# The first batch's loads and order, its weights' buffer, and the slots of all batches in a two-stage attention and gating kernel

## The chip, the cores and the metric

The kernel runs on one core of a Trainium2 chip. Its time is the device time in microseconds of one execution, and several executions give a median. The profile is of one execution; its times start at the first instruction.

## What is computed

For each of four batches, `x` is 12800 x 128 in f32. First 32 inducing vectors attend to all rows of `x` (softmax over 12800, giving `h`, 32 x 128), then every row of `x` attends to `h` (softmax over 32). The result goes through a gated block: a causal depthwise convolution of 5 taps and a sigmoid give the gate, a 128 x 128 product the value, and a second 128 x 128 product the output. The `moe_` weights arrive as f64.

```
def mab(q, kv):
    s = scale * (q @ kv.transpose(0, 2, 1))
    s = s - s.max(-1, keepdims=True)
    a = np.exp(s)
    a /= a.sum(-1, keepdims=True) + 1e-09
    return a @ kv
h = mab(I, x)
x = mab(x, h)
gate_pre += conv_w[k][None, None, :] * xp[:, k:k + S, :]   # k = 0..4
gate = 1.0 / (1.0 + np.exp(-gate_pre))
return (gate * (x @ w_val) @ w_out)
```

## The kernel before

A batch's 12800 rows are four strips (r = 0 to 3) of 3200, and a strip is cut into chunks c of up to 512 columns (`SIZES`): 128, 256, five of 512 and 256 in batch 0; 480, five of 512 and 160 in the others. A pair of a batch and a chunk covers all four strips side by side, so 4 x n rows.

Per batch there are these steps, each a function that adds operations to a plan:

- `load_xt` (L292) brings a chunk of `x` with channels on the partitions, 1024 KB for 512 columns; `load_xk` (L303) brings the same rows with tokens on the partitions and a column of ones. In batch 0, chunks 0 to 5 have no second load: `make_xk` (L315) transposes them on TensorE (L335) and ScalarE (L340) or VectorE (L342) copies them out.
- `s1` (L349): scores against the inducing vectors on TensorE (L359), copied from PSUM with a running maximum by VectorE (tile `ss`, L367).
- `gmax` (L371), in two halves `gm` and `gn`: the maximum of a group of chunks (`GROUPS`), across partitions by a small product (L385), and back by another (L399).
- `e1` and `h` (L412, L427): exponential on ScalarE, transpose on VectorE (`et`), and the product with the tokens (L437), summed into `H` by VectorE.
- `prep` to `prep_out` (L453 to L616): the groups' `H` are joined (L477) and normalised, `hT` is h transposed (L496), and from it and the weights come the gate's and value's weights `W` and the output's `wo`, each in two f16 halves.
- `s2` (L620): scores against `hT` (L633), then ten steps on VectorE, GpSimd and ScalarE that end in the softmax weights `P`, again in two f16 halves. The last are the cast (L682) and the subtraction on GpSimd (L687); for chunk 0 two memsets on GpSimd follow (L692, L693) that clear the halo of 32 columns.
- `rblock` (L722): one half-chunk of gate products (L707) and value products (L716), then tanh on ScalarE (L769) and gate times value on VectorE (L780).
- `halves` (L786): the result `tg` as two f16 halves: `gh` is cast by VectorE (L794) for strips 1 and 3 and by ScalarE (L796) for 0 and 2; `gl` is a subtraction on GpSimd (L802). `outp` (L806) multiplies with `wo` in three f16 products (L814 to L816), scales on ScalarE and stores.

TensorE runs in the order in which the plan was built: the list `START` for the beginning, then half-chunks of `rblock`, with the steps of the next batch put between them by slots (`FILL`, in half-chunks relative to the start of a batch, and `LEAD`, by how many half-chunks a chunk's `s2` comes ahead). The other engines' order is chosen by `Plan.lay`, which runs the plan forward with the durations in `COST` and takes the ready operation that is due first. SyncE's transfers are ordered in the same way. `BUFS` has the number of buffers for each name: four of `xk`, eleven of `xt`, five of `tg`, four PSUM banks `a` and one each of `g0` to `g3`.

The f64 weights are loaded as integers into a buffer of `xk` (L226) and converted on VectorE by eleven operations (L244 to L257) that work in the rest of that buffer.

Of the kernel before, what the change touches and what calls it, by code (L numbers as in the profile page):

```python
# [36 lines left out]
LAT = 0.12  # L37
PASSES = 6

COST = dict(  # L40
    s=0.867 / 512, h=0.052, unit=0.2135 / 512, out=0.68 / 512, switch=0.13,
    psum=(0.14, 1.05e-3), dve=(0.17, 1.02e-3), act=(0.16, 0.83e-3), pool=(0.19, 1.78e-3),
# [3 lines left out]
class Plan:  # L46
# [7 lines left out]
    def op(self, eng, dur, fn, deps=(), early=0.0, new=(), use=()):  # L54
        i = len(self.ops)
        self.ops.append(dict(eng=eng, dur=dur, fn=fn, deps=[d for d in deps if d is not None], early=early))
        for key in new:
            self.tiles.setdefault(key[0], []).append((i, key))
            assert key not in self.users, key
            self.users[key] = []  # L60
        for key in use:
            self.users[key].append(i)
        return i

    def order(self, pe):
# [38 lines left out]
        for i in pe:  # L104
            nominal[i] = t
            t += ops[i]["dur"]
# [10 lines left out]
    def lay(self, deps, succ, topo, nominal):  # L117
# [18 lines left out]
        while len(seq) < n:  # L136
# [12 lines left out]
            end[i] = start + ops[i]["dur"]  # L149
            free[e] = end[i]  # L150
# [23 lines left out]
def tile_kernel(ctx: ExitStack, tc: tile.TileContext, xt, xk, indT_in, w64, out):  # L174
# [16 lines left out]
    def PE(dur, fn, deps=(), new=(), use=()):  # L191
        i = plan.op("PE", dur, fn, deps, 0.0, new, use)
# [39 lines left out]
    i_const = op("POOL", 2.5, f_const)  # L232

    def weights(after):
        w = {}

        def start():
            w["w4"] = c_["wbuf"][:, K64:3 * K64].bitcast(I32).rearrange("p (a k) -> p a k", a=4)
# [3 lines left out]
            w["b"], w["t"], w["u"] = (w["w4"][:, i] for i in range(3))  # L242
            w["lo"] = w["w4"][:, 3].bitcast(F32)
# [16 lines left out]
        for f in ops:  # L260
            i = op("DVE", 0.37, f, [i], 0.0, [], [("xk", "w")])
# [8 lines left out]
        return op("DVE", 0.1, cmax, [i])  # L270
# [13 lines left out]

    def ago():
# [17 lines left out]
    def load_xk(b, c):  # L303
# [4 lines left out]
        def f():  # L308
            x = sb(pxk, key, [P, n, P + 1], F32, [P, 16, P + 1])
            nc.sync.dma_start(x, xk[b, :, o:o + n * (P + 1)].rearrange("p (i c) -> p i c", c=P + 1))  # L310

        ix[key] = op("SP", n * 66048 / BW, f, [ago()], 0.0, [key])


    def make_xk(b, c, eng):  # L315

        n = SIZES[b][c] // 32
        o = HALO // 32 if c == 0 else 0
        key = ("xk", b, c)
        last = []  # L320

        def ones():
            x = sb(pxk, key, [P, n, P + 1], F32, [P, 16, P + 1])
            G.memset(x[:, :, P:], 1.0)

        i0 = op("POOL", 0.15, ones, [], 0.0, [key])
        for g in range(0, n, 4):
# [9 lines left out]
            def ev(g=g, k=k, tk=tk, e=eng[g // 4 % len(eng)]):  # L337
                dst, src = st[key][:, g:g + k, :P], st[tk][:, :k, :]
# [6 lines left out]
            i = PE(0.109 * k + 0.05, tp, [ix["xt", b, c, 1], i_const], [tk], [("xt", b, c, 1)])  # L345
            last.append(op("ACT" if e == "S" else "DVE", 0.6, ev, [i, i0], 0.0, [], [tk, key]))
        ix[key] = op("NOP", 0.0, lambda: None, last)

    def s1(b, c):  # L349
        n = SIZES[b][c]  # L350
        o = HALO // 32 if c == 0 else 0
        key, ss, mx = ("a", "s1", b, c), ("ss", b, c), ("mx", b)
        new = c == 0

        def f():
            s = pt(key)
            x = st["xt", b, c, 1]
# [3 lines left out]
        i = PE(COST["s"] * n + COST["switch"], f, [ix["xt", b, c, 1], i_ind, i_const], [key], [("xt", b, c, 1)])  # L361
# [7 lines left out]
        ix[ss] = op("DVE", cost("psum", n) + 0.1, g, [i], 0.0, [ss] + [mx] * new, [key] + [mx] * (not new))  # L369

    def gmax(b, g):  # L371
# [9 lines left out]
        i0 = op("DVE", 0.12, f0, [ix["ss", b, c] for c in cs], 0.0, [m1], [("mx", b)])  # L381
# [5 lines left out]
        i1 = PE(0.35, f1, [i0, i_const], [key], [m1])  # L387
# [5 lines left out]
        i2 = op("DVE", 0.25, f2, [i1], 0.0, [mr], [key])  # L393

        def second():
# [5 lines left out]
            i4 = PE(0.3, f4, [i2], [key2], [mr])  # L401
# [6 lines left out]
            ix["ng", b, g] = op("DVE", 0.2, f5, [i4], 0.0, [("ng", b)] * (g == 0), [key2] + [("ng", b)] * (g > 0))  # L408
# [3 lines left out]
    def e1(b, g, c):  # L412
# [7 lines left out]
        i = op("ACT", cost("act", n) + 0.09, f, [ix["ng", b, g]], 0.0, [], [ss, ("ng", b)])  # L420
# [6 lines left out]
    def h(b, g, c):  # L427
        nb = SIZES[b][c] // 32
        cs = GROUPS[b][g]
        key, H = ("a", "h", b, c), ("H", b, g)  # L430

        def f():
            t = pt(key)
            e, x = st["et", b, c], st["xk", b, c]
            for i in range(nb):
                s = i % R
                T.matmul(t[32 * s:32 * s + 32, :P + 1], e[:, 32 * i:32 * i + 32], x[:, i, :],  # L437
                         start=i < R, stop=i >= nb - R)
# [10 lines left out]
        pre = [i] + ([ix[H]] if c != cs[0] else [])  # L449
        ix[H] = op("DVE", 0.28, acc, pre, 0.0, [H] * (c == cs[0]), [key] + [H] * (c != cs[0]))  # L450


    def prep(b):  # L453
# [9 lines left out]
        i0 = op("DVE", 0.25, f0, [ix["ng", b, g] for g in gs] + [i_const], 0.0, [f_], [("ng", b)])  # L463
        i0 = op("ACT", 0.25, lambda: S.activation(st[f_], st[f_], AF.Exp, scale=-1.0), [i0], 0.0, [], [f_])
# [6 lines left out]
        i0 = op("DVE", 0.15 * len(gs), f1, [i0], 0.0, Ds, [f_])  # L471
# [7 lines left out]
        i2 = PE(0.23 * len(gs), f3, [i0] + [ix[k] for k in Hs], [key], Hs + Ds)  # L479
# [7 lines left out]
        ix["hn", b] = op("DVE", 0.45, f4, [i2], 0.0, [("hn", b)], [key])  # L487

    def prep1(b):
# [5 lines left out]
        i = PE(0.2, f5, [ix["hn", b]], [key], [("hn", b)])  # L495
        ix["hT", b] = op("DVE", 0.2, lambda: V.tensor_copy(sb(pb, ("hT", b), [P, M]), st[key][:, :M]), [i], 0.0,  # L496
                         [("hT", b)], [key])

    def prep2(b):
# [7 lines left out]
        i4 = PE(0.3, f4, [ix["hT", b], iw], [key], [("hT", b)])  # L507
# [9 lines left out]
        i = op("DVE", 0.5, g0, [ix["hT", b], iw], 0.0, [gmx, cg], [("hT", b)])  # L517
# [19 lines left out]
        i = op("DVE", 0.6, g2, [i4], 0.0, [vmx, wv], [key])  # L537
# [6 lines left out]
        iv = op("DVE", 0.25, g3, [i, ih], 0.0, [], [wv, w2])  # L544
# [437 lines left out]
```

## Time and profile before

| what | us |
|---|---|
| median of 3 runs | 324.81 (323.74 to 325.12) |
| the profiled execution, its own time | 323.54 |
| its span, first to last instruction | 321.6 |
| DMA traffic over the span | 75.03 MB |
| `gl` on GpSimd, 116 operations | 121.3 busy |
| gate products on TensorE, 1740 | 119.4 busy |
| gate times value on VectorE, 116 | 65.7 busy |
| tanh and output scaling on ScalarE, 116 each | 70.4 and 69.6 busy |

A row of the list of groups reads: line, engine, operation, output and inputs, shape, count, then busy time in us, the mean in ns of one, and the idle time just before them. A row of the timeline reads: start, duration in us, engine, line, what it does, count, and in brackets the idle time before it and what ended that. A row of a stage has the stretch, its length and the busy us (and count) of TensorE's products, TensorE's weight loads, VectorE, ScalarE and GpSimd, then TensorE's granted clock, the DMA engines' share and GB/s. Busy times of single TensorE products overlap.

### The profile page before, as it was taken

To read this page: it belongs to the slowest core of one execution; us is meant where nothing else is said; L and a number is where in the kernel's file an instruction comes from. 1 tells how busy PE (TensorE), PEld (TensorE's weight loads), DVE (VectorE), ACT (ScalarE), POOL (GpSimd) and SP (SyncE) were. 2 spreads that over 40 slices of the span, in tenths; PEclk is the share of its full clock that TensorE was granted. 3 is DMA by queue.
4 is the path that set the end of the run, shared out by engine and by line. 5 is a ranking of instruction groups with operands and counts; after the bars stand their busy time and mean duration, and the time that the engine had idled before them with its cause. 6 is when DMAs were issued, how large, how long until landed. Compare 5 with 4: busy or idle time off the path is not lost.

```text
span 321.6 us, 10290 instructions
## 1 busy us (share of the span) xinstructions
PE 297.3 (92%) x4112; PEld 141.1 (44%) x4112; DVE 259.9 (81%) x629; ACT 214.8 (67%) x406; POOL 210.1 (65%) x233
## 2 busy tenths in 40 slices
PE   8996769999998999999999999999898989999894
PEld 3665535643442446433443446334444334333241
DVE  1578596789988998888998889898999988988452
ACT  3453024577866678679765785788657777879595
POOL 1000044579758685889758777886877698999573
PEclk9997795999999999999999999999997999999798
DMA  7996990863999619958999299523221322233334
GB/s 296 427 416 246 423 418 11 314 231 116 346 408 413 257 67 349 402 204 306 287 412 391 86 316 385 186 92 129 96 102 67 132 110 94 106 124 130 130 133 172
DMA packets 24527, 75.03 MB, mean 233 GB/s; under 512 B 2848, under 2 KB 7456, under 8 KB 19488
## 3 DMA queue, kind: packets, MB, share of 16 engines
q1 hardware_dynamic: 24336, 74.37, 60.8%
q8 instruction: 32, 0.52, 0.7%
q14 instruction: 15, 0.12, 0.1%
q10 hardware_dynamic: 144, 0.02, 0.0%
HBM read 48.16 MB, written 26.21 MB: 231 GB/s over the span
## 4 chain that ended last, share of the span: by engine, by line
PE 61%; DVE 20%; DMA 7%; POOL 4%; issue 4%; ACT 2%; SPq 1%; DVEq 0%; ACTq 0%
PE g L707 21%; PE a L814 6%; PE a L437 6%; PE a L633 6%; PE a L716 6%; PE a L816 5%; PE a L815 5%; DMA wbuf<-in_w_dram 5%; PE a L359 4%; DVE tg L780 3%; POOL gl L802 3%; DVE gh L794 2%; DVE e L639 2%; DVE ss L367 2%; DMA xk<-in_xk_dram 2%
## 5 line engine op out<-in xcount | busy, mean ns | idle before, releaser
L802 POOL TENSOR_TENSOR gl<-tg,gh 128x512 f16<-128x512 f32 (+4 forms) x116 | 121.3, 1056 | 33.6 <-ACT gh L796 24.7
L707 PE MATMUL g<-P,W 32*128 32x512 f16 (+4 forms) x1740 | 119.4, 354 | 5.1 <-POOL P L687 3.6
L769 ACT ACTIVATE tg<-g,gsc 128x512 f32<-128x512 f32 (+4 forms) x116 | 70.4, 627 | 20.9 <-PE g L707 18.9
L707 PEld LDWEIGHTS <-W 32*128 32x128 f16 x1740 | 54.7, 94 | 55.5 <-issue 26.3
L780 DVE SCALAR_TENSOR_TENSOR tg<-tg,a 128x512 f32<-128x512 f32 (+4 forms) x116 | 65.7, 599 | 10.9 <-PE a L716 9.7
L821 ACT ACTIVATE os<-a,osc 128x512 f32<-128x512 f32 (+4 forms) x116 | 69.6, 629 | 3.5 <-PE a L816 1.0
L796 ACT CAST gh<-tg 128x512 f16<-128x512 f32 (+4 forms) x58 | 32.5, 560 | 24.5 <-DVE tg L780 24.4
L716 PE MATMUL a<-P,W 32*128 32x512 f16 (+4 forms) x348 | 45.3, 352 | 1.1 <-DVE W L568 0.7
L814 PE MATMUL a<-gh,wo 128*128 128x512 f16 (+4 forms) x116 | 41.5, 359 | 1.5 <-DVE ss L367 0.8
L816 PE MATMUL a<-gl,wo 128*128 128x512 f16 (+4 forms) x116 | 40.6, 352 | 0.9 <-POOL gl L802 0.8
L815 PE MATMUL a<-gh,wo 128*128 128x512 f16 (+4 forms) x116 | 40.8, 354 | 0.0
L687 POOL TENSOR_TENSOR P<-pt,P 128x512 f16<-128x512 f32 (+2 forms) x29 | 30.6, 1055 | 14.9 <-ACT P L682 14.7
L794 DVE CAST gh<-tg 128x512 f16<-128x512 f32 (+4 forms) x58 | 37.0, 638 | 1.1
L670 POOL TENSOR_TENSOR e<-e,z 128x512 f32<-128x512 f32 (+2 forms) x29 | 27.8, 957 | 15.1 <-DVE z L664 12.2
L437 PE MATMUL a<-xk,et 128*32 128x129 f32 x800 | 30.1, 299 | 4.6 <-DVE et L423 2.1
L650 POOL TENSOR_TENSOR e<-e,m 128x512 f32<-128x512 f32 (+2 forms) x29 | 27.7, 955 | 5.2 <-DVE m L644 4.2
L437 PEld LDWEIGHTS a<-xk,et 128*32 128x32 f32 x800 | 25.3, 119 | 12.4 <-issue 6.4
L359 PE MATMUL a<-xt,indT 128*32 128x512 f32 (+4 forms) x232 | 29.4, 562 | 0.5 <-DMA xt<-in_xt_dram 0.5
L633 PE MATMUL a<-xt,hT 128*32 128x512 f32 (+2 forms) x232 | 28.3, 564 | 0.6 <-DVE hT L496 0.6
L682 ACT CAST P<-pt 128x512 f16<-128x512 f32 (+2 forms) x29 | 16.4, 565 | 18.4 <-DVE pt L676 18.3
L639 DVE STREAM_TRANSPOSE e<-a 128x512 f32<-128x512 f32 (+2 forms) x29 | 18.5, 638 | 10.8 <-PE a L633 10.8
L367 DVE TENSOR_SCALAR_CACHE_REDUCE ss<-a 128x512 f32<-128x512 f32 (+4 forms) x29 | 17.4, 599 | 9.4 <-PE a L359 9.2
(105 smaller groups left out, 314.9 us busy)
## 6 DMA issues: line engine op xcount, KB each, us to landing
xt<-in_xt_dram SPq DMA_DIRECT2D x23, 1024.0 KB, 8.8
out_dram<-os SPq DMA_DIRECT2D x80, 256.0 KB, 2.2
xk<-in_xk_dram SPq DMA_DIRECT2D x16, 1032.0 KB, 8.9
xk<-in_xk_dram SPq DMA_DIRECT2D x3, 967.5 KB, 6.8
out_dram<-os SPq DMA_DIRECT2D x12, 240.0 KB, 2.0
xt<-in_xt_dram SPq DMA_DIRECT2D x4, 320.0 KB, 8.7
xt<-in_xt_dram SPq DMA_DIRECT2D x2, 512.0 KB, 9.9
out_dram<-os SPq DMA_DIRECT2D x8, 128.0 KB, 5.6
```

What stands on the lines that cost most here:

```text
L437: T.matmul(t[32 * s:32 * s + 32, :P + 1], e[:, 32 * i:32 * i + 32], x[:, i, :], start=i < R, stop=i >= nb - R)
L633: T.matmul(s[32 * r:32 * r + 32, :n], st["hT", b], x[:, :, r, :], start=True, stop=True)
L707: T.matmul(st[f"g{r}", b, c][:, :n], st["W", b][q, w, k, :], st[("P1", "P2")[e]][q, o:o + n], start=u == 0, stop=u == len(taps) - 1)
L716: T.matmul(st["a", "v", b, c, r][:, :n], st["W", b][q, w, TAPS, :], st[("P1", "P2")[e]][q, o:o + n], start=u == 0, stop=u == 2)
L769: S.activation(t[:, :n], st[f"g{r}", b, c][:, :n], AF.Tanh, scale=st["gsc", b])
L780: V.scalar_tensor_tensor(t[:, :n], t[:, :n], 1.0, st["a", "v", b, c, r][:, :n], ALU.add, ALU.mult)
L794: V.tensor_copy(t, st[tg][:, :n])
L802: G.tensor_tensor(sb(pw, g2, [P, 512], F16)[:, :n], st[tg][:, :n], st[g1][:, :n], ALU.subtract)
L814: T.matmul(t, w[:, 0], st[g1][:, :n], start=True, stop=False)
L815: T.matmul(t, w[:, 1], st[g1][:, :n], start=False, stop=False)
L816: T.matmul(t, w[:, 0], st[g2][:, :n], start=False, stop=True)
L821: S.activation(sb(pw, os, [P, 512])[:, :n], st[key][:, :n], AF.Copy, scale=st["osc", b])
```

## The change

The plan is built from other numbers and another list, and some steps are changed. What changes in the code beside the numbers:

- In batch 0 chunks 0 and 1 share one `xt` tile and one `xk` tile (`shares`, `xt_of`).
- The loads are named in `START` (`l`), and those of the start leave in the order of that list (`sp` chains them, `behind`). Before, all of batch 0's loads were in the plan first and the planner chose.
- Chunks 4, 5 and 6 of batch 0 are loaded in tokens, 1032 KB each; chunks 0 to 3 and 7 are transposed. Before, 6 and 7 were loaded. `XEV` names the engine of each copy.
- The f64 weights and the conversion's scratch stand in three of the `tg` buffers.
- Chunk groups of batch 0 are 0 to 2, 3 and 4, and 5 to 7.
- `wo`'s cast goes from VectorE to ScalarE and its subtraction to GpSimd.
- The halo is cleared by one small memset in the sums of the softmax on VectorE, in place of the two on GpSimd at the end of the chain.
- In batch 1 VectorE casts only strip 2 of `gh`, ScalarE the three others (`HIV`).
- The very last chunk has no halves: one f32 product with `wof` (the output's weights before they are split).
- A load may be issued six half-chunks ahead (`AHEAD`), before three.
- The planner has a latency for each engine, an overlap of successive operations, and durations that differ from before by some hundredths.

`idle`, `QUICK` and the argument `bank` are added but not used.

```
 def f_wload():
-    t = c_["wbuf"] = pxk.tile([P, 8 * (P + 1)], I64, name="wbuf", tag="xk", bufs=BUFS["xk"])
-    c_["raw"] = t[:, :K64]
+    c_["raw"] = pw.tile([P, K64], I64, name="raw", tag="tg", bufs=BUFS["tg"])
     nc.sync.dma_start(c_["raw"], w64)
...
+def sp(dur, fn, new, use=()):
+    i = op("SP", dur, fn, [ago()], 0.0, new, use, behind=queue[-1:])
+    if not blocks:
+        queue.append(i)
+    return i
...
+def shares(b, c):
+    two = SIZES[b][0] + SIZES[b][1] + HALO <= 512
+    return (0, SIZES[b][0] // 32) if two and c == 1 else (c, 0)
...
-        i = op("DVE", 0.7, f3, [i2], 0.0, [("osc", b), ("wof", b)], [key, vmx])
+        i = op("DVE", 1.0, f3, [i2], 0.0, [("osc", b), ("wof", b)], [key, vmx])
+        i = op("ACT", 0.3, lambda: S.copy(sb(pb, ("wo", b), [P, 2, P], F16)[:, 0], st["wof", b]), [i], 0.0,
+               [("wo", b)], [("wof", b)])
         def f4():
-            w = sb(pb, ("wo", b), [P, 2, P], F16)
-            V.tensor_copy(w[:, 0], st["wof", b])
-            V.tensor_tensor(w[:, 1], st["wof", b], w[:, 0], ALU.subtract)
+            G.tensor_tensor(st["wo", b][:, 1], st["wof", b], st["wo", b][:, 0], ALU.subtract)
...
 def sm():
     ...
     V.reciprocal(z, z)
+    if c == 0:
+        V.memset(z[:M, 0], 0.0)
...
-    if c == 0:
-        def edge():
-            G.memset(st[p1][:M, :HALO], 0.0)
-            G.memset(st[p2][:M, :HALO], 0.0)
...
 def hi():
     t = sb(pw, g1, [P, 512], F16)[:, :n]
-    if r % 2:
+    if r in HIV[b]:
         V.tensor_copy(t, st[tg][:, :n])
...
 def outp(b, c, r):
+    if (b, c) == seqs[-1]:
+        def f():
+            T.matmul(pt(key)[:, :n], st["wof", b], st["tg", b, c, r][:, :n], start=True, stop=True)
...
-GROUPS = [[[0, 1, 2], [3, 4, 5], [6, 7]]] + [[[0, 1, 2], [3, 4, 5, 6]]] * 3
+GROUPS = [[[0, 1, 2], [3, 4], [5, 6, 7]], [[0, 1, 2], [3, 4, 5, 6]], [[0, 1, 2], [3, 4, 5, 6]], [[0, 1, 2], [3, 4, 5, 6]]]
 START = [
+    (0, "l", 0), (0, "l", 1), (0, "s1", 0), (0, "s1", 1), (0, "l", 2), (0, "x", 0), (0, "s1", 2), (0, "x", 2),
...
+XEV = ["SSVV", "SSSS", "SSSS", "SVSS", "VVSS", "SVVS", "SSVV", "SSVS"]
+HIV = [(1, 3), (2,), (1, 3), (1, 3)]
-BW = 400e3
+BW = 424e3
-LEAD = [2, 2, 2, 3]
-AHEAD = 3
+LEAD = [[5.5, 1.5, 4, 7, 4.5, 7.5, 6, 4.5], [2, 3.5, 3.5, 5.5, 6.5, 1.5, 5], [1.5, 2, 3, 7, 8, 3, 6], [5, 6, 3.5, 8.5, 4, 4, 2.5]]
+AHEAD = 6
```

SyncE's queue at the start of the program. A row is a line, the transfer and its shape (2048 columns are a chunk of 512, 2064 its tokens); 1935 are the tokens of batch 1's first chunk. Before:

```order
L299 DMA xt<-in_xt_dram 128x640
L299 DMA xt<-in_xt_dram 128x1024
L299 DMA xt<-in_xt_dram 128x2048 x5
L228 DMA wbuf<-in_w_dram 128x261
L299 DMA xt<-in_xt_dram 128x1024
L299 DMA xt<-in_xt_dram 128x2048 x3
L310 DMA xk<-in_xk_dram 128x2064
L310 DMA xk<-in_xk_dram 128x1032
L310 DMA xk<-in_xk_dram 128x1935
```

And now:

```order
L330 DMA xt<-in_xt_dram 128x640
L330 DMA xt<-in_xt_dram 128x1024
L330 DMA xt<-in_xt_dram 128x2048
L236 DMA raw<-in_w_dram 128x261
L330 DMA xt<-in_xt_dram 128x2048 x3
L330 DMA xt<-in_xt_dram 128x1024
L330 DMA xt<-in_xt_dram 128x2048
L341 DMA xk<-in_xk_dram 128x2064 x3
L330 DMA xt<-in_xt_dram 128x2048 x4
L341 DMA xk<-in_xk_dram 128x1935
```

The weights moved from eighth to fourth place, three loads of tokens stand where two stood, and batch 1's chunks of `xt` stand behind them instead of ahead.

TensorE from the last groups of h products of batch 0 to its first scores against `hT` (`xk,et` are the h products, `identf,m` and `ones,mr` the two halves of a group's maximum, `H,D` the joining, `identf,hn` the transpose to `hT`). Before:

```order
L437 MATMUL a<-xk,et 32x129 x16
L385 MATMUL a<-identf,m_418 1x128
L437 MATMUL a<-xk,et 32x129 x16
L399 MATMUL a<-ones,mr 32x1 x4
L437 MATMUL a<-xk,et 32x129 x40
L477 MATMUL a<-H,D 32x129 x3
L359 MATMUL a<-xt,indT 32x480 x4
L493 MATMUL a<-identf,hn 128x32
L633 MATMUL a<-xt,hT 32x160 x4
```

And now:

```order
L392 MATMUL a<-xt,indT 32x512 x4
L472 MATMUL a<-xk,et 32x129 x16
L418 MATMUL a<-identf,m_388 1x128
L432 MATMUL a<-ones,mr 32x1 x4
L472 MATMUL a<-xk,et 32x129 x56
L512 MATMUL a<-H,D 32x129 x3
L528 MATMUL a<-identf,hn 128x32
L540 MATMUL a<-hT,w 128x32
L392 MATMUL a<-xt,indT 32x480 x4
L671 MATMUL a<-xt,hT 32x160 x4
```

The last maximum now stands ahead of 56 blocks of h products instead of 40, right behind the scores of chunk 5, and batch 1's first scores moved behind the transpose.

GpSimd near the end of the program, where the last two pieces of P of batch 3 are made (`P` the subtraction that ends a chunk, `e<-e,m` and `e<-e,z` earlier steps of `s2`, `gl` the lower half of the gated value). Before:

```order
L802 TENSOR_TENSOR gl<-tg,gh 128x512
L670 TENSOR_TENSOR e<-e,z 128x512
L802 TENSOR_TENSOR gl<-tg,gh 128x512 x3
L687 TENSOR_TENSOR P_97<-pt,P_96 128x512
L670 TENSOR_TENSOR e<-e,z 128x160
L687 TENSOR_TENSOR P_97<-pt,P_96 128x160
L802 TENSOR_TENSOR gl<-tg,gh 128x512 x8
L802 TENSOR_TENSOR gl<-tg,gh 128x160 x4
```

And now:

```order
L713 TENSOR_TENSOR e<-e,z 128x512
L840 TENSOR_TENSOR gl<-tg,gh 128x512 x2
L730 TENSOR_TENSOR P_97<-pt,P_96 128x512
L840 TENSOR_TENSOR gl<-tg,gh 128x512 x2
L691 TENSOR_TENSOR e<-e,m_5734 128x160
L840 TENSOR_TENSOR gl<-tg,gh 128x512 x2
L713 TENSOR_TENSOR e<-e,z 128x160
L840 TENSOR_TENSOR gl<-tg,gh 128x512 x2
L730 TENSOR_TENSOR P_97<-pt,P_96 128x160
L840 TENSOR_TENSOR gl<-tg,gh 128x512 x6
```

Behind the last wide P stood eight wide `gl`, now twelve; the last chunk's four narrow ones are gone.

More of the change, by code (lines that the diff above doesn't have):

```diff
@@ L36 @@
 SCALE = 1.0 / math.sqrt(P)
-LAT = 0.12
 PASSES = 6
+LAT = dict(PE=0.3, DVE=0.06, ACT=0.045, POOL=0.09, SP=0.05, NOP=0.0)
+OVER = dict(DVE=0.075, ACT=0.105, POOL=0.035)
+OWN = 0.035
+SWITCH = 0.09
 COST = dict(
-    s=0.867 / 512, h=0.052, unit=0.2135 / 512, out=0.68 / 512, switch=0.13,
-    psum=(0.14, 1.05e-3), dve=(0.17, 1.02e-3), act=(0.16, 0.83e-3), pool=(0.19, 1.78e-3),
+    s=0.867 / 512, h=0.052, unit=0.2135 / 512, out=0.655 / 512,
+    psum=(0.145, 1.04e-3), dve=(0.175, 1.01e-3), cast=(0.17, 0.85e-3), act=(0.195, 0.836e-3),
+    pool=(0.17, 1.72e-3), lo=(0.16, 1.96e-3),
 )
@@ L105, in order @@
             nominal[i] = t
-            t += ops[i]["dur"]
+            t += ops[i]["dur"] + ops[i].get("turn", 0.0)
         best = None
@@ L148, in lay @@
             at[i] = start
-            end[i] = start + ops[i]["dur"]
-            free[e] = end[i]
+            end[i] = start + ops[i]["dur"] + ops[i].get("turn", 0.0)
+            free[e] = end[i] - OVER.get(e, 0.0)
             if e == "SP":
@@ L754, in f @@
                         fn(*a)
-            return PE(sum(COST["unit"] * max(SIZES[w[1]][w[2]] for w in row) for row in todo if row) + COST["switch"] / 2,
-                      f, deps, new, use)
+            return PE(sum(COST["unit"] * max(SIZES[w[1]][w[2]] for w in row) for row in todo if row) + 0.02,
+                      f, deps, new, use, "rows", 0.34)
         i0 = part(range(3), newv)
@@ L796, in hi @@
                 S.copy(t, st[tg][:, :n])
-        i = ix[g1] = op("DVE" if r % 2 else "ACT", cost("dve" if r % 2 else "act", n), hi, [ix["gv", b, c, r]], 0.0,
+        i = ix[g1] = op("DVE" if r in HIV[b] else "ACT", cost("cast" if r in HIV[b] else "act", n), hi, [ix["gv", b, c, r]], 0.0,
                         [g1], [tg])
@@ L836, in tile_kernel, with idle, f, S1 @@
     PE(0.43 * WARM, warm_up, [i_zero], [("a", "warm")])
-    n0 = len(SIZES[0])
-    for c in range(n0):
-        load_xt(0, c)
-    def S1(b, c):
-        load_xt(b, c)
-        load_xk(b, c)
-        s1(b, c)
+    def idle(b, k, n):
+        key = ("g3", "idle", k)
+        def f():
+            t = pt(key)
+            for _ in range(n):
+                T.matmul(t, c_["zero"][:, :P], c_["zero"], start=True, stop=True)
+        PE(0.216 * n, f, [], [key])
+    def S1(b, c, bank="a"):
+        if ("xt", b, c, 1) not in ix:
+            load_xt(b, c)
+        if b and ("xk", b, c) not in ix:
+            load_xk(b, c)
+        s1(b, c, bank)
     def Hs(b, g, c):
```

227 lines of the change are left out of this document (130 added, 97 removed), and 28 rows, old and new, of tables (FILL, START).

## The prediction

> **What bounds the kernel now.** I read the page first: the span, the engines' shares, the granted clock.
>
> ```profile
> span 321.6 us, 10290 instructions
> PE 297.3 (92%) x4112; PEld 141.1 (44%) x4112; DVE 259.9 (81%) x629; ACT 214.8 (67%) x406; POOL 210.1 (65%) x233
> PEclk9997795999999999999999999999997999999798
> ```
>
> TensorE is busy 92% of the span, but the clock row shows dents, and a busy TensorE at half clock does half the work. So I cut the span by stages next (busy time of each engine, then clock, DMA share and GB/s): from the first batch's first matmul to its h transposed (38.7), from there to the first long row of gate products (49.8), the first two chunks (60.3), then the rest in four; then three stretches of low clock.
>
> ```profile
> 4.70:38.70 34.00, 28.62 (x386) 19.84 (x385) 20.29 (x70) 12.40 (x24) 0.38 (x3) 0.90 0.93 379
> 38.70:49.80 11.10, 8.04 (x116) 3.31 (x116) 10.22 (x41) 2.50 (x6) 5.07 (x11) 0.87 0.87 365
> 49.80:60.30 10.50, 10.50 (x223) 7.24 (x226) 7.30 (x20) 5.82 (x15) 3.40 (x5) 0.65 0.25 84
> 60.30:120.00 59.70, 57.39 (x815) 25.62 (x815) 53.61 (x130) 41.61 (x79) 45.40 (x49) 1.00 0.72 275
> 120.00:180.00 60.00, 59.58 (x869) 27.27 (x857) 52.74 (x126) 45.62 (x84) 46.45 (x46) 1.00 0.87 321
> 180.00:240.00 60.00, 58.05 (x853) 27.53 (x850) 54.97 (x124) 43.66 (x82) 45.39 (x48) 1.00 0.50 181
> 240.00:299.00 59.00, 53.63 (x672) 21.71 (x673) 50.61 (x98) 45.87 (x85) 50.27 (x52) 0.97 0.30 111
> 46.90:57.10 10.20, 9.49 (x136) 5.02 (x140) 7.22 (x23) 4.17 (x10) 3.82 (x6) 0.50 0.14 57
> 244.90:248.40 3.50, 3.50 (x33) 1.90 (x26) 3.05 (x7) 1.84 (x4) 2.28 (x4) 0.52 0.02 8
> 299.30:302.70 3.40, 3.40 (x21) 1.05 (x14) 1.94 (x4) 2.71 (x5) 2.25 (x3) 0.52 0.02 7
> ```
>
> Three regimes. Up to 38.7 TensorE idles 5.4 us (34.0 less 28.62). From 38.7 to 49.8 VectorE is the bound (10.22 of 11.1). From 60.3 to 299 TensorE is the bound: it idles 2.3 + 0.4 + 2.0 + 5.4 = 10.1 us, with VectorE close behind (88 to 92%). The three cold stretches hold 16.4 us of busy TensorE at half clock, so up to 8.2 us of lost work.
>
> **Startup, the main term.** The chain of waits (start, us, what) tells what the first 37 us wait for.
>
> ```profile
> 4.04 15.46 DMA wbuf<-in_w_dram
> 28.14 4.92 DMA xk<-in_xk_dram
> 33.19 2.81 PE a L437 x48
> 36.00 0.89 PE a L477 x5
> ```
>
> The weights are the eighth transfer and land at 19.50; their conversion holds an `xk` buffer, so the token loads of chunks 6 and 7 start only at 28.14. Rows of the timeline, with what a wait ended on in brackets:
>
> ```profile
> 8.45 1.06 PE L359 MATMUL a<-xt,indT 128*32 128x512 f32 x8 [0.46 <-DMA xt<-in_xt_dram]
> 9.45 1.97 PE L335 MATMUL g<-identf,xt 128*128 128x128 f32 x16
> 18.65 1.09 PE L437 MATMUL a<-xk,et 128*32 128x129 f32 x32
> 27.20 0.43 DVE L257 SCALAR_TENSOR_TENSOR w<-wbuf 128x261 f32<-128x261 int32 x1
> 33.19 2.81 PE L437 MATMUL a<-xk,et 128*32 128x129 f32 x48 [2.04 <-DMA xk<-in_xk_dram]
> 38.47 0.19 DVE L496 COPY hT<-a 128x32 f32<-128x32 f32 x1
> 20.00:25.00 5.00, 4.42 (x50) 2.37 (x42) 4.93 (x18) 2.01 (x4) 0.10 (x1) 1.00 1.01 422
> ```
>
> The conversion ends at 27.63 and `hT` is there at 38.66, 5.6 us after the last tokens landed (33.06). In the change the weights have a buffer of their own and all of the batch's transfers leave back to back. The third one, as before, is used at 8.45; at 422 GB/s a 1024 KB transfer takes 2.5 us and the 261 KB of weights 0.63. Then 261 KB, three of 1024, one of 512, one of 1024 and three token loads of 1032 KB end at 8.45 + 0.63 + 7.5 + 1.25 + 2.5 + 7.5 = 27.8. With the same 5.6 us behind, `hT` comes at 33.4: 5.3 earlier, the best case. TensorE may be later than the data: its products up to `hT` are scores of 7.0 us (L359: 1.06 for 512 columns, less for narrow ones), 52 transposes at 0.123 (1.97 for 16), 6.4, instead of 76, h products of 100 blocks at 1.09 for 16, 6.8, and 2.5 of small ones; 22.7 us from 4.7 on, so 27.4 without waits. But the third group of maxima now takes chunks 5 to 7; walked through in its order with these durations (score of chunk 5 at 24, maximum and its return at 27.3, exponential and transpose of chunk 6 to 29.0, then three h products of 2.7 and the 2.7 behind them), `hT` comes at 34.5. Cold clock on those products, as at 33.19 (2.81 for 24 blocks where 1.64 is full speed), would add up to 1.9. I take 34.5: **-4.2**, bounds -5.3 to -2.3.
>
> **Ramp.** Behind `hT` VectorE makes the first tiles of P, one per chunk (L676, the transposed weights):
>
> ```profile
> 44.31 0.34 DVE L676 STREAM_TRANSPOSE pt<-e 128x160 f32<-128x160 f32 x1
> 47.47 0.43 DVE L676 STREAM_TRANSPOSE pt<-e 128x256 f32<-128x256 f32 x1
> 56.96 0.70 DVE L676 STREAM_TRANSPOSE pt<-e 128x512 f32<-128x512 f32 x1
> 49.84 1.14 PE L707 MATMUL g<-P,W 32*128 32x128 f16 x30
> 60.26 0.28 PE L716 MATMUL a<-P,W 32*128 32x256 f16 x2
> ```
>
> They end at hT + 6.0, + 9.2 and + 19.0. In the new order VectorE has more ahead of them (the second chunk's scores, two scans of batch 1): adding up the rows I get hT + 8, + 12.5 and + 18. But before, the first two tiles lay ready: the long row of gates started at 49.84 (hT + 11.2), behind a wait for a maximum and scores at half clock, and the block that needs the third tile at 60.26. The new row stands behind one more score, and the second tile is wanted right after it, at about hT + 13.5; the block of the third starts near hT + 20.6 against hT + 21.6. I take **-1.0**; bounds +2.3 (the first gates are later by that, and nothing is regained) and -4.7 (none of the 9.49 us of the cold stretch is cold).
>
> Whether the clock falls in the new ramp decides much of this. The windows ahead of two of the falls:
>
> ```profile
> 43.50:46.90 3.40, 1.90 (x24) 0.89 (x24) 3.30 (x16) 1.02 (x2) 1.39 (x5) 0.99 1.02 431
> 241.50:244.90 3.40, 2.07 (x50) 0.86 (x42) 3.21 (x9) 3.31 (x7) 2.82 (x3) 0.99 0.41 151
> ```
>
> It fell at 46.9 after TensorE had been busy 1.90 of 3.4 us, and at 244.9 after 2.07: in neither was it silent for 3.4 us. [...] I leave the term at -1.0.
>
> **From 60 us on.** Nothing is removed from TensorE here; only waits can go, 10.1 us of them, and half of 6.9 us at low clock. Two waits with their reason, and one that the change may multiply:
>
> ```profile
> 298.90 1.43 PE L707 MATMUL g<-P,W 32*128 32x512 f16 x16 [1.91 <-POOL P L687]
> 259.34 0.99 PE L707 MATMUL g<-P,W 32*128 32x480 f16 x20 [1.42 <-POOL P L693]
> 118.14 0.38 PE L814 MATMUL a<-gh,wo 128*128 128x512 f16 x1 [0.80 <-DVE ss L367]
> ```
>
> At 298.9 the gates wait for GpSimd, which did three `gl` subtractions ahead of the last wide P. In the new order that P stands four `gl` further ahead, so this wait goes, and with it the cold stretch behind it (1.7). At 259.3 the last step is the memset of the halo (L693), which becomes a memset of 32 partitions on VectorE in the sum of the exponentials. VectorE, late in most other gaps, loses work:
>
> ```profile
> L794 DVE CAST gh<-tg 128x512 f16<-128x512 f32 x40 | 27.1, 678 | 0.6
> L612 DVE TENSOR_TENSOR wo<-wof,wo 128x128 f16<-128x128 f32 x4 | 3.5, 876 | 0.1
> L342 DVE COPY xk<-g 128x512 f32<-128x512 f32 x4 | 2.7, 686 | 1.0 <-PE g L335 1.0
> ```
>
> In batch 1 one `gh` cast per chunk goes to ScalarE (some 6.4 of 0.68: 4.3), `wo`'s subtraction to GpSimd (3.5) and its cast to ScalarE, three copies go (2.1): 10 of 259.9 us. ScalarE takes about 4 of it where it is busy 45.6 of 60, which covers it; were that cover gone, 7 casts of 0.6 would cost 4. The per-batch slots bring scores forward by up to 8 half-chunks. What the whole re-ordering is worth no row shows; the bounds are all idle and cold time of this stretch (10.1 + 3.4 = -13.5) and a wait like that at 118.14 at a third of the 42 scores that follow the startup (+11). Nearest to the rows is the named part: 1.9 + 1.7 at 299, 0.5 at 259 and a tenth of the rest. I take **-4.5**.
>
> **Tail.** In the last chunk (160 columns) the halves go, and TensorE takes the product in f32.
>
> ```profile
> 316.37 0.31 ACT L796 CAST gh<-tg 128x160 f16<-128x160 f32 x1
> 316.76 0.93 POOL L802 TENSOR_TENSOR gl<-tg,gh 128x160 f16<-128x160 f32 x2 [0.94 <-ACT gh L796]
> 318.25 0.39 ACT L821 ACTIVATE os<-a,osc 128x160 f32<-128x160 f32 x1 [0.24 <-DMA out_dram<-os]
> ```
>
> From 316.37 to 317.69 cast and subtraction go; one f32 product of 160 columns costs 1.06 x 160/512 = 0.33 against three of 0.07, so two more add 0.25. **-1.0**, bounds -1.4 and -0.3.
>
> **Sum.** -4.2 - 1.0 - 4.5 - 1.0 = -10.7 against the profiled run's own time of 323.54 us (its span and 1.94 around it), so 312.8; the median shown is 324.81 and the runs spread over 1.4, so I say **313.0**.
>
> **Rivals.**
> - *Only the first 50 us and the tail gain.* Waits leave one place and come back elsewhere, as TensorE's 97% between 60 and 299 suggests. 323.5 - 6.2 = 317.3. Against it: the wait at 298.9 has a clear cause that goes. Chance 0.20.
> - *The clock stays up.* Without the cold stretches of the ramp and at 244.9 and 299.3: 313 - 3.7 - 1.5 = about 307.8. [...] Chance 0.10.
> - *The ramp takes the startup back.* VectorE is full there (10.22 of 11.1), and work moved ahead of the P tiles delays them: if the third tile is ready at its old time, the 5.2 of startup and ramp are gone, and if waits in the middle return as well, 323.5 - 1.0 = 322.5, no change. Chance 0.07.
> - *Slower: scores brought forward block TensorE's queue.* A score needs one of the four `a` banks, freed by VectorE; as at 118.14, outputs and gates queue behind it. With 42 scores after the startup it decides from 6.2/42 = 0.15 us each that the startup gain is spent; at the 0.4 of half the measured 0.80 it costs 17: 334. Chance 0.08. For it: VectorE at 88 to 92%; against it: VectorE loses 10 us.
> - The forecast itself: 0.55.
>
> **Range and chances.** 306.5 holds the warm clock, 320.5 the case without a gain in the middle and with a cold startup (317.3 + 1.9, and the spread); left out is the deepest re-ordering gain, the no-change and the slower case. 0.5% (1.6 us) is about what a measurement of this kernel can tell from no change. Faster 0.55 + 0.20 + 0.10 = 0.85; same 0.07; slower 0.08.
>
> **What would show it.** Startup: the third token load lands near 28, `hT` is written at 33.4 to 36.4, and no TensorE wait on `xk` is over 1 us. Ramp: the first block with the third P starts at 54 to 57. Middle: idle TensorE between 60 and the last ten us falls from 10 to 5 or 7, and no cold stretch stands before the last chunk. Tail: one f32 product, 1 us less between the last value product and the last store. I am wrong if `hT` comes after 37, or if waits of TensorE on scans (`ss`) and transposes (`e`) grow past 10 us.

## The result, and the profile after

| | us | ratio to before, 95% |
|---|---|---|
| before, on the same chip | 324.44 median (323.74 to 325.12) | |
| the change | 314.28 median (313.37 to 314.78) | 0.9684 (0.965 to 0.9717) |
| the change's profiled execution, its own time | 313.37 | |

The change is faster by 3.2% (by 2.4% when it was measured again, on another chip: see the experiments). Medians here and below are over all executions, ratios leave out those more than 1.5% above the fastest of their kernel. From the first page of its profile, span, engines and granted clock:

```profile
span 311.6 us, 10239 instructions
PE 287.3 (92%) x4084; PEld 136.0 (44%) x4084; DVE 250.9 (81%) x613; ACT 218.3 (70%) x412; POOL 208.2 (67%) x224
PEclk9799999998999999999999999999999999999999
```

TensorE's busy time fell by 10.0 us (297.3 to 287.3), its idle time not at all: 24.3 us before and after. Some 3 us of it are 24 transposes fewer (0.123 each); the rest is mostly work no longer done at half clock, at which TensorE was busy for 23.1 us before and 6.8 after: in the change an output product of 512 columns starts 0.22 us behind the one ahead of it at full clock (from 68.04) and 0.43 at half clock (from 76.00). The stages of the change, as shown of before:

```profile
4.70:33.70 29.00, 22.74 (x349) 14.85 (x345) 17.53 (x64) 11.20 (x21) 0.24 (x2) 0.94 1.01 410
33.70:52.50 18.80, 16.03 (x305) 7.83 (x306) 18.17 (x65) 8.50 (x21) 9.78 (x15) 1.00 1.01 419
60.00:305.60 245.60, 235.58 (x3285) 106.07 (x3279) 206.44 (x464) 189.82 (x351) 190.68 (x188) 0.99 0.60 214
38.10:41.50 3.40, 2.25 (x35) 0.73 (x24) 3.29 (x11) 1.73 (x4) 1.07 (x2) 1.00 1.03 427
72.20:75.60 3.40, 1.45 (x37) 0.96 (x34) 3.37 (x7) 2.58 (x5) 2.20 (x3) 1.00 0.99 313
75.60:79.00 3.40, 3.40 (x30) 1.62 (x32) 2.43 (x7) 1.74 (x3) 2.52 (x3) 0.50 0.58 230
```

VectorE is busy in nearly all of the ramp (18.17 of 18.8), with TensorE's clock now full (1.00); before, it was busy for 17.5 of the ramp's 21.6. Between 60 us and the last value products TensorE still idles 10.0 us (245.6 less 235.58). The timeline marks where the stages end: the third token load's issue and its products, the first block with the third P, the last value products, the last scaling.

```profile
21.63 0.33 SPq L341 DMA_DIRECT2D xk<-in_xk_dram  x1
29.20 2.41 PE L472 MATMUL a<-xk,et 128*32 128x129 f32 x80 [0.87 <-PE a L472]
52.45 0.44 PE L753 MATMUL a<-P,W 32*128 32x256 f16 x2
305.58 0.38 PE L753 MATMUL a<-P,W 32*128 32x160 f16 x6
308.55 0.39 ACT L870 ACTIVATE os<-a,osc 128x160 f32<-128x160 f32 x1 [0.74 <-DMA out_dram<-os]
```

The bracket behind the products names another product of TensorE, but the load landed at 29.01, 7.4 us after its issue. `hT` is in the chain of waits (start, us, what):

```profile
33.55 0.20 DVE hT L531
```

| stage ends with | before | after | the stage alone | predicted |
|---|---|---|---|---|
| `hT` written | 38.7 | 33.7 | -4.9 | -4.2 |
| first block with the third P | 60.3 | 52.5 | -2.9 | -1.0 |
| last value products begin | 315.3 | 305.6 | -1.9 | -4.5 |
| end of the span | 321.6 | 311.6 | -0.3 | -1.0 |

The sum is right (-10.0 against -10.7) and three of its terms are not. In the list of waits the ones on GpSimd's P are gone from the middle, and a new one stands there. Before (who waits, for whom, us in total, times, longest):

```profile
PE g L707 <- POOL P L687: 3.6, 3, 1.9
PE g L707 <- POOL P L693: 1.4, 1, 1.4
ACT os L821 <- DMA out_dram<-os: 1.0, 3, 0.5
```

And after:

```profile
ACT os L870 <- DMA out_dram<-os: 6.0, 6, 1.9
PE a L753 <- ACT os L870: 3.2, 4, 1.5
PE g L744 <- POOL P L730: 0.3, 1, 0.3
```

ScalarE scales an output into one of four `os` buffers, and a buffer is free when its store has landed. The timeline of one such wait, on TensorE, ScalarE and SyncE's queue:

```profile
144.16 0.37 PE L753 MATMUL a<-P,W 32*128 32x512 f16 x1 [1.52 <-ACT os L870]
143.42 0.69 ACT L870 ACTIVATE os<-a,osc 128x512 f32<-128x512 f32 x1 [1.88 <-DMA out_dram<-os]
130.79 2.02 SPq L341 DMA_DIRECT2D xk<-in_xk_dram  x3
134.44 10.03 SPq L875 DMA_DIRECT2D out_dram<-os  x5
```

The change's chain of waits has four long pieces that are stores:

```profile
84.79 10.15 DMA out_dram<-os
134.44 8.90 DMA out_dram<-os
145.53 8.63 DMA out_dram<-os
190.78 8.00 DMA out_dram<-os
```

A store issued at 134.44, behind three loads of tokens issued from 130.79 on, lands 8.90 us later, where the median store of 256 KB takes 2.5. The value products of 144.16 need a PSUM bank that the waiting scaling would have freed. Loads and stores share SyncE's queue here. The three loads land 6.5, 9.4 and 9.1 us after their issue, the last near 141.5, and the store after them, at 143.34; from 134.4 to 142.0 the DMA engines are busy for 0.98 of the time. That the store is late because of the loads ahead of it is the author's reading of these times; no run shows it apart. Late stores are not new, though: before, 25 of the 116 stores took more than 6 us to land (8.7 at most), in the change 17 (10.1 at most). New is that ScalarE wants the buffers back while they are out: it waited 1.0 us for them before and 6.0 after.

### The profile page after: what moved, and what is told of

The parts are those of the page before. It is cut to its first block, busy times and chain, and to the rows that moved or that the text cites. A ratio compares the mean times of both kernels' runs of the same rounds, so it can differ in the third digit from the quotient of the medians.

```text
span 311.6 us, 10239 instructions
## 1 busy us (share of the span) xinstructions
PE 287.3 (92%) x4084; PEld 136.0 (44%) x4084; DVE 250.9 (81%) x613; ACT 218.3 (70%) x412; POOL 208.2 (67%) x224
## 4 chain that ended last, share of the span: by engine, by line
PE 50%; DVE 15%; DMA 15%; ACT 9%; issue 6%; POOL 4%; POOLq 1%; SPq 0%; ACTq 0%; DVEq 0%
PE g L744 15%; DMA out_dram<-os 12%; PE a L671 5%; PE a L472 5%; PE a L753 5%; PE a L859 5%; PE a L861 4%; PE a L860 4%; ACT tg L806 3%; ACT os L870 3%; PE a L392 3%; DVE tg L817 3%; DMA xt<-in_xt_dram 2%; PE g L368 2%; POOL gl L840 2%
## 5 line engine op out<-in xcount | busy, mean ns | idle before, releaser
L840 POOL TENSOR_TENSOR gl<-tg,gh 128x512 f16<-128x512 f32 (+4 forms) x112 | 118.9, 1073 | 41.4 <-ACT gh L834 30.2
L744 PE MATMUL g<-P,W 32*128 32x512 f16 (+4 forms) x1740 | 116.6, 345 | 2.4 <-ACT P L725 1.2
L806 ACT ACTIVATE tg<-g,gsc 128x512 f32<-128x512 f32 (+4 forms) x116 | 67.8, 625 | 3.8 <-PE g L744 3.2
L834 ACT CAST gh<-tg 128x512 f16<-128x512 f32 (+4 forms) x63 | 35.7, 568 | 24.1 <-DVE tg L817 23.7
L859 PE MATMUL a<-gh,wo 128*128 128x512 f16 (+4 forms) x112 | 40.2, 361 | 0.1
L860 PE MATMUL a<-gh,wo 128*128 128x512 f16 (+4 forms) x112 | 39.9, 358 | 0.0
L832 DVE CAST gh<-tg 128x512 f16<-128x512 f32 (+4 forms) x49 | 30.3, 619 | 1.2
L472 PE MATMUL a<-xk,et 128*32 128x129 f32 x800 | 27.6, 279 | 3.9 <-ACT tg L806 1.9
L472 PEld LDWEIGHTS a<-xk,et 128*32 128x32 f32 x800 | 22.3, 111 | 14.1 <-issue 3.3
L697 ACT ACTIVATE e<-e 128x512 f32<-128x512 f32 (+2 forms) x29 | 16.7, 575 | 16.6 <-POOL e L691 16.6
L451 ACT ACTIVATE ss<-ss,ng 128x512 f32<-128x512 f32 (+4 forms) x29 | 17.7, 659 | 5.4 <-DVE ng L439 5.4
(106 smaller groups left out, 309.2 us busy)
```

The source lines that it names most:

```text
L744: T.matmul(st[f"g{r}", b, c][:, :n], st["W", b][q, w, k, :], st[("P1", "P2")[e]][q, o:o + n], start=u == 0, stop=u == len(taps) - 1)
L806: S.activation(t[:, :n], st[f"g{r}", b, c][:, :n], AF.Tanh, scale=st["gsc", b])
L840: G.tensor_tensor(sb(pw, g2, [P, 512], F16)[:, :n], st[tg][:, :n], st[g1][:, :n], ALU.subtract)
L859: T.matmul(t, w[:, 0], st[g1][:, :n], start=True, stop=False)
L860: T.matmul(t, w[:, 1], st[g1][:, :n], start=False, stop=False)
```

## The experiments

Three theories stood for the missing middle and its cause: the new wait on output buffers eats a gain that the new slots bring; the slots bring nothing; what gains is elsewhere, in the planner's numbers or in the moved operations. Ratios are to the kernel before on the same chip. The first four runs are from one chip, the later ones from another, and the change itself came to 0.9684 and to 0.9761 in its two measurements; so a difference of under 1% between the two groups is not shown by the times alone. The planner lays out the other engines anew in most of these kernels, so their order can differ beyond the edit; where it does not, the text says so.

**Six output buffers** (no engine's order changes):

```
-BUFS = dict(... os=4 ...)
+BUFS = dict(... os=6 ...)
```

> The changed kernel with six output buffers (os) instead of four, the order of every engine the same. Theory A (the waits that the new order took from GpSimd's P came back as waits for output buffers: a store lands late behind loads, ScalarE's scaling waits, an `a` bank stays taken, TensorE waits): TensorE's waits on ScalarE's scaling (3.2 us in the changed kernel, four of them) and ScalarE's on stores (6.0 us) go, and the kernel is 2 to 4 us faster than the changed one, some 311. Rival B (these waits lie beside others that are as long): less than 1 us.

308.27 us, 0.9542 (0.949 to 0.9594), clear of the change's interval. No wait on a store is left in its profile, and of TensorE's value products one waits for the scaling:

```profile
PE a L753 <- ACT os L870: 0.3, 1, 0.3
```

TensorE's other work keeps its order, so the wait was worth about 1.4% (0.9684 to 0.9542, from two measurements).

**The slots of before** in the change:

```
-FILL, LEAD = (of the change)
+FILL, LEAD = (of before)
```

> The changed kernel with the slots of before for batches 1 to 3 and for every s2 (FILL and LEAD), the start, the buffers and the moved operations as changed. It measures what the new slots are worth. Theory A (start and clock made nearly all of the gain, the new slots about 2 us): 315 to 318. Rival (the slots carry half of the gain): 320 or more. If the slots cost more than they bring: 313 or less.

310.08 us, 0.9613 (0.9568 to 0.9657): without its new slots the change is at least as fast. The waits on output buffers are smaller there:

```profile
ACT os L870 <- DMA out_dram<-os: 2.1, 5, 0.8
PE a L753 <- ACT os L870: 0.8, 2, 0.6
```

**Halves in the last chunk**, so three f16 products again; the planner then reorders other engines too:

```
-                if (b, c) != seqs[-1]:
-                    halves(b, c, r)
+                halves(b, c, r)
```

> The changed kernel with the two halves and three f16 products for the very last chunk again. My term of the prediction: 1.0 us slower, 315.3. Theory A (the last store waits for an output buffer anyway, so the shorter chain is hidden): within 0.5 us of the changed kernel; in its profile the time from the last value products to the end is 6.0 to 6.5 us.

312.42 us, 0.9659 (0.9596 to 0.9722): no difference from the change that can be told. From the last value products to the end it takes 5.9 us, the change 6.0. On its chip this is the nearest to the change, and the change with six buffers is 1.2% below it.

**The weights' buffer alone**, in before:

```
-    t = c_["wbuf"] = pxk.tile([P, 8 * (P + 1)], I64, name="wbuf", tag="xk", bufs=BUFS["xk"])
+    c_["raw"] = pw.tile([P, K64], I64, name="raw", tag="tg", bufs=BUFS["tg"])
```

> The kernel of before with one thing changed: the f64 weights and their conversion stand in tg buffers, so that no xk buffer waits for them. If the weights' hold on the buffer was what made the tokens late: chunk 6's load starts near 20 instead of 28, hT comes 1.5 to 3 us earlier than at 38.7, and the kernel is 1 to 3 us faster than before. Rival (the products of chunk 3 hold the next buffer until 28 as well, and chunk 7's tokens are as late): under 0.7 us.

322.2 us, 0.9973 (0.993 to 1.0016). In its profile the first token load is issued at 19.9 in place of 28.1, as the theory had it, and `hT` is there at 36.7, 1.9 us earlier. But profiles of the kernels below that keep the weights in `xk` and the start of before have `hT` at 37.2 to 38.8, so 0.5 to 2.1 us are the buffer's. The time is 0.3% less, which cannot be told from none.

**The change again**, on another chip, beside the next three:

> The changed kernel as it is, for comparison with the others on one chip: 0.965 to 0.972 of before.

315.77 us (312.3 to 318.47), 0.9761 (0.9688 to 0.9835): a smaller gain than expected, though the intervals meet. In its profile the ramp has one stretch of 3.4 us at half clock (at 43.0) where the first profile of the same kernel has none, and the ramp is 19.1 us long, there 18.7.

**Slots of before and six output buffers:**

> The changed kernel with the slots of before (FILL and LEAD) and six output buffers. With the old slots only 0.6 us of TensorE's idle time ended on ScalarE's output scaling, against 3.2 with the new ones. If the new slots' loss is these waits (theory A), six buffers bring at most 1 us here, and this kernel and the change with six buffers come out within 1 us of each other, at 0.953 to 0.960 of before. Rival (the old slots are better by themselves, whatever the buffers): 2 us or more under the change with six buffers, below 0.950.

308.65 us (307.85 to 309.2), 0.9576 (0.9536 to 0.9616). With six buffers the new slots (0.9542) and the old ones can't be told apart, so what the slots cost with four is, as far as the times tell, the wait on buffers. These two kernels beat both before and the change.

**The start of before too** (`START`, `GROUPS`, `XEV` and slots; what is left is the planner's numbers, moved operations, the weights in `tg`, the tile that chunks 0 and 1 share, the last product, `AHEAD`):

> The changed kernel with the start of before (START, the chunk groups, chunks 6 and 7 loaded in tokens) and the slots of before. What is left of the change: the planner's durations and latencies, weights in tg buffers, wo and the halo moved, batch 1's casts, the last chunk's product, AHEAD. It splits the gain of the old-slots kernel (0.961 of before) in the start and the rest. Theory A (the start with its clock made most): 0.982 to 0.992. Rival (the planner's numbers and the moved operations made most): 0.970 to 0.978. In the profile the wait for P at the end of batch 3 (1.9 us before) is gone, since P stands ahead of the last gl already here; if it is there, the new slots removed it.

312.34 us, 0.9711 (0.9664 to 0.9758). So most of the gain does not come from the new list of the start nor from the slots. Against 0.9613, from the other chip, the new start is worth about 1%, 3 us; in the profiles it is 4.4, of which 3.1 by `hT` and 1.8 in the ramp. The wait for the last wide P of batch 3 is gone here already, so the new slots did not remove it.

**A warm ramp in before**, by 13 products of zeros in the two holes of the ramp:

```
+        for _ in range(n):
+            T.matmul(t, c_["zero"][:, :P], c_["zero"], start=True, stop=True)
...
-    (0, "W", 1), (0, "po"), (1, "s1", 2), (0, "pp"),
+    (0, "W", 1), (0, "z", 0, 8), (0, "po"), (1, "s1", 2), (0, "pp"), (0, "z", 1, 5),
```

> The kernel of before with 13 products of zeros on TensorE in the two gaps behind hT (8 ahead of the output maximum, 5 behind the last step of the list), nothing else; the result is the same. If the cold stretch from 46.9 to 57.1 is set by the half-empty window ahead of it and costs TensorE what it says: the stretch is gone or shorter and the kernel is 2 to 4 us faster, 0.988 to 0.994 of before. Rival (VectorE bounds the ramp, the clock costs nothing there): 0.997 to 1.003, with the clock up.

323.26 us, 1.0022 (0.9988 to 1.0056). Its profile by stages shows the ramp's cold stretch of 10.2 us gone, and one at 257 in place of that at 244.9:

```profile
46.90:57.10 10.20, 10.01 (x259) 6.51 (x262) 8.86 (x25) 6.36 (x17) 5.45 (x8) 1.00 0.41 145
257.00:260.60 3.60, 3.60 (x30) 1.34 (x32) 1.33 (x4) 3.01 (x7) 2.38 (x4) 0.53 0.22 77
```

The ramp is 19.3 us long in place of 21.6, but the stage behind it is 1.6 longer and the last one 0.6. It is not the clock alone that differs: between 42 and 87 us the planner gave VectorE, ScalarE and GpSimd another order. So this kernel gains nothing that can be measured, and the worth of a warm ramp in the time stays open.

**Moved operations undone**, on the kernel with the start and slots of before: what is left is the planner's numbers, the weights in `tg`, the tile that chunks 0 and 1 share, and `AHEAD`. The last chunk has its halves and three products again too.

```
-HIV = [(1, 3), (2,), (1, 3), (1, 3)]
+HIV = [(1, 3), (1, 3), (1, 3), (1, 3)]
...
-                G.tensor_tensor(st["wo", b][:, 1], st["wof", b], st["wo", b][:, 0], ALU.subtract)
+                V.tensor_copy(w[:, 0], st["wof", b])
+                V.tensor_tensor(w[:, 1], st["wof", b], w[:, 0], ALU.subtract)
...
-            if c == 0:
-                V.memset(z[:M, 0], 0.0)
+                G.memset(st[p1][:M, :HALO], 0.0)
+                G.memset(st[p2][:M, :HALO], 0.0)
```

> The kernel with the start and the slots of before came to 0.971 of the time of before. Here its moved operations are undone as well: wo is cast and subtracted on VectorE, the halo is cleared by two memsets on GpSimd, VectorE casts strips 1 and 3 in batch 1 too, and the last chunk has its halves and three products. What is left of the change is the planner's durations, latencies and overlap, the weights in the tg buffers, and loads issued six half-chunks ahead. Theory 1, the order of VectorE, ScalarE and GpSimd that follows from the planner's numbers carries the gain: 0.968 to 0.977, and the wait of the gates for the last wide P at the end of batch 3 (1.9 us before) stays below 0.4 us. Theory 2, it is VectorE's relief of 10 us: only the startup of 3.4 us is left, 0.985 to 0.992, and VectorE's waits come back.

319.23 us, 0.9875 (0.9829 to 0.9922): the size of theory 2. Yet the waits are not those of before. The wait of 1.9 us for the last wide P is gone, as theory 1 had it. Between 60 and 290 us the list has a single wait on P, for the halo's memset that this kernel has again (L734), and waits on VectorE's transpose `e` and on the output scaling:

```profile
PE a L862 <- DVE e L677: 1.9, 2, 1.3
PE a L757 <- ACT os L873: 1.3, 3, 0.8
PE g L748 <- POOL P L734: 0.7, 1, 0.7
```

**And loads three half-chunks ahead** in that kernel:

```
-AHEAD = 6
+AHEAD = 3
```

> The kernel of the run above, with loads issued at most three half-chunks ahead, as before. If the distance of the loads matters, TensorE waits for xt and xk again and the time goes back by 2 to 4 us: 0.978 to 0.99. If the planner's durations alone carry it: within 0.4% of the run above.

318.57 us, 0.9861 (0.9791 to 0.9931): how far ahead loads may be issued makes no difference here that can be told.

**Moved operations alone**, in before (the same edits the other way round, without the last product):

> The other way round: the kernel before with the moved operations alone (wo's cast to ScalarE and subtraction to GpSimd, the halo by a memset on VectorE, one cast per chunk of batch 1 from VectorE to ScalarE); planner's numbers, loads, start and slots as before. Theory 1, the planner's numbers carry the gain: 0.992 to 1.002. Theory 2, VectorE's relief carries it: 0.975 to 0.985. The halo's memset alone should take the wait of 1.42 us at the start of batch 3's gates: up to 0.5 us.

321.62 us, 0.9939 (0.99 to 0.9978). Relief of VectorE alone does not carry the gain either. The waits for the halo (1.4 us) and for the last wide P (1.9) are gone in its profile, but the wide P ahead of that is waited for, 0.9 us, and another one at 157.4, 0.6.

**Six output buffers in before:**

> The kernel before with six output buffers in place of four; no engine's order changes. If the wait on output buffers belongs to the change's early loads alone: 0.998 to 1.002, since ScalarE waits 1.0 us for them in before and TensorE not at all. If four buffers bound the kernel before as well: 0.985 to 0.993.

322.91 us, 1.0009 (0.9976 to 1.0043). Four buffers did not bound the kernel before; the change made them a bound.

Where the kernels stand along the way shows how the parts go together. Start in us of the first tanh of some of the 58 half-chunks (counted from 0), and the end of the span, from one profile each. "Numbers" is the kernel with the moved operations undone (it has the weights in `tg` too), "moved" the moved operations alone, "both" the one with the start of before (and the single last product), "with new start" the one with the slots of before:

| half-chunk | before | numbers | moved | both | with new start | the change | change, six buffers |
|---|---|---|---|---|---|---|---|
| 8 | 83.9 | 78.6 | 82.9 | 79.3 | 74.7 | 82.9 | 82.6 |
| 20 | 145.1 | 142.3 | 143.1 | 141.1 | 136.7 | 140.9 | 139.7 |
| 38 | 235.5 | 235.1 | 237.2 | 230.9 | 226.6 | 237.0 | 233.6 |
| 52 | 294.7 | 294.6 | 296.9 | 289.5 | 285.2 | 289.2 | 285.8 |
| end | 321.6 | 317.5 | 320.6 | 312.7 | 308.3 | 311.6 | 307.5 |

The planner's numbers gain 5.3 us by half-chunk 8, hold 2.8 at 20 and have lost all but 0.4 at 38; then the last six half-chunks, where the wait for P and the cold stretch behind it are gone, bring 4 again. With the moved operations the early gain stays (4.6 at 38). The same profiles by stages (us):

| stage | before | numbers | moved | both | with new start | the change | change, six buffers |
|---|---|---|---|---|---|---|---|
| start to `hT` | 38.7 | 37.2 | 37.5 | 35.3 | 32.2 | 33.7 | 33.4 |
| ramp: `hT` to the block with the third P | 21.6 | 18.8 | 21.8 | 21.1 | 19.3 | 18.7 | 18.7 |
| half clock in the ramp | 10.2 | 3.4 | 10.2 | 10.2 | 3.4 | 0 | 0 |
| middle: from there to the last value products | 255.0 | 255.5 | 255.0 | 250.0 | 250.5 | 253.1 | 250.0 |
| TensorE idle in the middle | 10.4 | 10.8 | 11.6 | 6.6 | 6.8 | 10.0 | 8.0 |
| tail: from there to the end | 6.3 | 6.1 | 6.3 | 6.4 | 6.2 | 6.0 | 5.4 |

Neither the numbers nor the moved operations shorten the middle alone; together they take 5 us off it. The rows of the middle, of before, the numbers, the moved operations and both:

```profile
60.30:315.30 255.00, 244.64 (x3373) 108.62 (x3369) 220.45 (x492) 190.20 (x353) 198.53 (x202) 0.99 0.58 217
55.91:311.45 255.54, 244.72 (x3373) 108.88 (x3369) 222.53 (x492) 190.22 (x353) 197.15 (x201) 1.00 0.59 211
59.31:314.33 255.02, 243.47 (x3371) 107.83 (x3368) 216.28 (x484) 193.71 (x363) 197.50 (x199) 1.00 0.59 217
56.40:306.37 249.97, 243.40 (x3371) 108.95 (x3369) 213.98 (x481) 192.40 (x362) 195.81 (x196) 1.00 0.60 216
```

The sums over four stages from 60 to 290 us, for the numbers alone:

```profile
sum 230.00, PE 219.80 PEld 98.59 DVE 205.13 ACT 168.36 POOL 173.84; mean PE 54.95 PEld 24.65 DVE 51.28 ACT 42.09 POOL 43.46
```

and with the moved operations:

```profile
sum 230.00, PE 224.15 PEld 100.44 DVE 202.80 ACT 175.13 POOL 179.99; mean PE 56.04 PEld 25.11 DVE 50.70 ACT 43.78 POOL 45.00
```

TensorE idles 10.2 us there in the one (230 less 219.80) and 5.85 in the other, while VectorE does less and ScalarE more.

## Why the prediction came out

**Startup: right.** -4.9 against -4.2. The third token load was issued at 21.63 and its products waited 0.87 us for it, until 29.2; `hT` came 4.5 later. TensorE was busy for 22.74 us in this stage, as the working had it (22.7). The weights' buffer alone gave 0.5 to 2.1 of it in a profile. In the time the new list is worth about 3 us (0.9711 to 0.9613, over two chips).

**Ramp: mechanism right, size too small.** The term "-1.0" kept cold stretches in the new ramp; none came in this profile, and one of 3.4 us in the other profile of the change. Over the fourteen profiles at hand the ramp's length goes with its clock: 21.1 to 21.8 us in the five with 6.8 to 10.2 us at half clock, 18.0 to 19.3 in the nine with 3.4 or none. So the -2.9 fits the clock better than the order of the steps, which differs within both groups; that the clock makes all of it is not shown: the two profiles of the change, one with 3.4 cold us in the ramp and one with none, are 0.4 apart. How much of it is in the medians stays open too: the warm ramp in before was no faster.

**From 60 us on: the step that failed.** "1.9 + 1.7 at 299, 0.5 at 259 and a tenth of the rest" counted waits that go and none that comes. The named waits went: P is waited for 0.3 us in all, and no cold stretch stands before the last chunk. But idle time between 60 us and the last value products stayed at 10 where 5 to 7 were forecast, since output buffers became a bound, 3.2 us on TensorE. With six buffers the stage runs from 52.1 to 302.1, 250.0 us, against 255.0 before and 253.1 in the change: -5.0, of which the buffers took 3.1. So the rival in which waits "come back elsewhere" happened for over half of this term.

That -5.0 is near the forecast does not make its sum right. With the planner's numbers alone, and with the moved operations alone, the wait of 1.9 us and both cold stretches of the middle are gone, and the middle is no shorter (255.5 and 255.0, with TensorE idle 10.8 and 11.6 in place of 10.4): with the numbers the last six half-chunks gain 4.0, but the lead at their start has fallen from 5.3 to 0.1. Only with both does idle time fall to 6.6 and the middle to 250.0. So the two need each other there, in profiles of one execution each: 255.0 to 255.7 in the six kernels with neither or one of them, 256.7 in that with products of zeros; 250.0 to 250.5 in the three with both and the old slots and in the change with six buffers. In the times the planner's numbers with the weights' buffer bring 1.25% (in the profile all of it ahead of the middle and in the tail), the moved operations 0.6%, and both together 2.9%; the 1% beyond the sum is about as large as the intervals. "The per-batch slots" bring nothing that can be measured with six buffers and cost 0.7 to 1.5% with four, by measurements on different chips.

**Tail: sized wrongly.** "From 316.37 to 317.69 cast and subtraction go" is true, but the last scaling waits 0.74 us for a store's buffer (0.24 before), and a store, issued at 309.0, ends the program. -0.3 of -1.0 was left, and taking the halves back changed nothing. In both kernels with six buffers and the single product the tail is 5.4 us, against 6.0 with six buffers in before: so the term comes near its size, -0.9, where no buffer is waited for.

**Rivals.** Slower by blocked `a` banks: waits of TensorE behind `ss` and `e` stay below 1 us in all. Warm clock: the ramp stayed warm in the first profile and one other stretch (75.6) did not; it was the right rival for the ramp, yet the time is not its 307.8. The ramp did not take the startup back: the block with the third P began at 52.5, 7.8 us earlier.

## What to carry to other kernels

- A new order should be read for how soon it wants back what is out on a queue: single stores took up to 8.7 us before and 10.1 after, with a median of 2.2 and 2.5, but ScalarE waited 1.0 us for their buffers in the old order and 6.0 in the new one, and two more buffers gave 1.4% there and nothing before.
- When new durations, moved work and new positions come in one change, try each alone: the part that looked largest in the code (slots) gained nothing, and two that look like bookkeeping (the planner's durations, and a few moved operations) took 5 us off the middle together and nothing alone.
- A sum that comes out right can hold three wrong terms; compare the stages' ends, not only the end.

## What the hardware showed that was not expected

- TensorE went to half clock after windows of 3.4 us in which it was busy 1.45 (at 72.2), and before 1.90 (at 43.5) and 2.07 us (at 241.5), and kept its clock after 2.25 (at 38.1). A busy TensorE did not bring the clock back at once: the ramp of before stayed at half clock for 10.2 us with TensorE busy 9.49 of them. Nor is busy time the whole of it: in the change the clock stayed full (1.00) for the 6.8 us behind a window with 1.77 (at 223.4).
- The same start differs between executions: TensorE took up the third transfer of `xt` at 9.37 us in the change's profile (after 2.84 us of waiting) and at 9.00 (1.78) with six output buffers, where no engine's order is other.
- Single executions of one program are up to 2% apart (before: 319.7 to 326.3 us over two chips), so a gain of a few us at one place of one profile, as with the warm ramp, need not be in the time.
